# The first x chunk's 1/std on ScalarE and VectorE in place of Pool, with GELU's table loaded behind the last statistics

## The chip, the cores and the metric

The kernel runs on one core of a Trainium2 chip. The metric is the device time of one execution in microseconds (us). Engines are named as in the profile: PE is TensorE (PEld its weight loads), DVE is VectorE, ACT is ScalarE, POOL is GpSimd, SP issues most of the transfers. Times inside an execution count from the start of its span. Runs are called by their labels; "before" and "after" are the two kernels of the change.

The change concerns the first 7 us of 697.

## The reference, cut to what matters

`x` has 2048 tokens of 1024 elements, in 16 chunks of 128 tokens (one token to a partition). It is normalised twice; the doubly normalised `h` feeds a token-mixing MLP, the singly normalised one an attention block.

```python
def _layernorm(x, axis=-1, eps=1e-05):
    m = jnp.mean(x, axis=axis, keepdims=True)
    v = jnp.var(x, axis=axis, keepdims=True)
    return (x - m) / jnp.sqrt(v + eps)
# in _B_ref: h = _layernorm(xn); u = gelu(einsum('bsd,sf->bdf', h, w1) + b1); y = einsum('bdf,fs->bds', u, w2) + b2
# xn = _layernorm(x); return x + _A_ref(xn, ...) + _B_ref(xn, ...)      (A attention, B MLP)
```

The MLP contracts over tokens, so its first matmuls can start as soon as chunk 0 of `h` and the first rows of `w1` are there. They then need one more chunk of `h` every 8 matmuls.

## The kernel before: the parts that matter

`h` of chunk c is `(x - mean) * rs`, with `rs` the power -0.5 of the variance plus a constant `E_H`. Even chunks have their statistics from VectorE (`bn_stats`, two halves, then `bn_aggr`), odd ones from two passes of ScalarE. A string gives the order in which work is put on the engines: D and d are VectorE statistics (D all of a chunk, d its first half, d' the second half and `bn_aggr`), A and A' ScalarE's two passes, S is `rs`, h is the scaling, C the bias columns. Each engine gets its own list from this string; in the traces VectorE and ScalarE take theirs in that order.

```python
    NORM_ORDER = (["D0 A1 S0 d2 h0 A1' A3 S1 d2' h1"] +
                  [f"S{c} d{c + 2} h{c} A{c + 1}' A{c + 3} S{c + 1} d{c + 2}' h{c + 1}" for c in range(2, 14, 2)] +
                  ["S14 h14 A15' S15 C h15"])

    def rstd(self, c):                       # "S"
        ...
        fw.op("dve", ... tensor_scalar(var, ..., E_H, op0=ALU.mult, op1=ALU.add) ...)
        fw.op("pool", ... tensor_tensor(rs, var, self.expo[:, 0:1], op=ALU.pow) ...)

    def early_hidden(self, c0, c1, bank_groups):       # 8 matmuls for each chunk, 4 for each half of h
        ...
            reads = self.R_w1e[c0:c1] + self.R_w1s[0:2] + self.R_hh[banks[0] % 2][c0:c1]
```

## Time and profile before

The three runs took 697.14, 697.40 and 697.45 us.

| what | value | view |
|---|---|---|
| span of the profiled execution | 695.2 us | page |
| TensorE busy | 685.3 us | page, part 1 |
| matmul's share of the chain that ended last | 98% | page, part 4 |
| first real matmul | 6.83 us | timeline |

The page of before, part 1 (busy us, share of the span, number of instructions) and part 4 (the chain of waits that ended last, by engine and by line):

```profile
PE 685.3 (99%) x4746; PEld 326.5 (47%) x4830; DVE 257.2 (37%) x581; ACT 280.2 (40%) x333; POOL 100.1 (14%) x156
...
PE 98%; issue 1%; DMA 1%; DVE 0%; SPq 0%
PE ps_all L194 98%; DMA xin<-in_A_x_dram 1%; SPq L216 0%; DVE ln_st L617 0%; DVE h L656 0%; DVE fin L1050 0%; PE ps_all L200 0%
```

Once the matmuls have begun they bound everything; a change to the normalisation pays only if they begin earlier and are then fed in time. The timeline of before around their beginning (start us, length us, engine, line, operation, output and inputs, count; in brackets the idle time before and what ended it):

```profile
5.05 0.21 DVE L620 BATCH_NORM_AGGREGATE ln_mv<-ln_st 128x2 f32<-128x12 f32 x1
5.29 0.15 DVE L639 TENSOR_SCALAR ln_mv<-ln_mv 128x1 f32<-128x1 f32 x1
5.53 0.55 POOL L641 TENSOR_TENSOR ln_rs<-ln_mv,expo 128x1 f32<-128x1 f32 x1 [3.96 <-DVE ln_mv L639]
5.67 0.69 DVE L617 BATCH_NORM_STATS2 ln_st<-xin 128x6 f32<-128x512 bf16 x1 [0.23 <-DMA xin<-in_A_x_dram]
6.29 0.72 DVE L656 TENSOR_SCALAR h<-xin,ln_mv,ln_rs 128x512 bf16<-128x512 bf16 x2
6.80 3.15 PEld L194 LDWEIGHTS ps_all<-h,w1early 128*128 128x128 bf16 x16 [2.00 <-DMA w1early<-in_B_w_dram]
6.83 17.43 PE L194 MATMUL ps_all<-h,w1early 128*128 128x512 bf16 x79 [1.51 <-DVE h L656]
6.92 0.14 DVE L639 TENSOR_SCALAR ln_mv<-ln_sm 128x1 f32<-128x1 f32 x1
7.14 0.55 POOL L641 TENSOR_TENSOR ln_rs<-ln_mv,expo 128x1 f32<-128x1 f32 x1 [1.07 <-DVE ln_mv L639]
7.83 0.68 DVE L656 TENSOR_SCALAR h<-xin,ln_mv,ln_rs 128x512 bf16<-128x512 bf16 x2
```

The first five lines are chunk 0: statistics, the added constant, Pool's power, then `h`, with a `bn_stats` of chunk 2 squeezed in front of `h`. The last three are the add, power and `h` of chunk 1. Its first half ends at 8.19, and the matmuls of chunk 1 begin at 8.55, without a gap behind the eight of chunk 0: `h` is ready about 0.2 us before it has to be, as a matmul starts some 0.15 us after the end of its `h` (the first ones here: 6.69 to 6.83).

### The profile page before, as it was taken

The page shows a single profiled execution, that of the slowest core. Times are in us where ns is not written, and L with a number is a line of the kernel's source. Part 1 is how long each engine was busy: PE and PEld are TensorE (multiplying, and loading weights), DVE is VectorE, ACT ScalarE, POOL GpSimd, SP SyncE. Part 2 cuts the span into 40 slices and gives each one's busy share as a digit, 9 for nine tenths or more (in the row PEclk, how much of TensorE's full clock was granted, in tenths as well). Part 3 has the DMA queues.
Part 4 walks back from the last instruction along what each step waited for, and adds up shares of the span by engine and source line. Part 5 has one row for each costly group of instructions (what it writes and reads, how often), then busy time and mean ns, then how long its engine had stood idle before and what let it go on. Part 6 is the DMA issues. An engine that isn't in the chain of part 4 may idle for free.

```text
span 695.2 us, 11228 instructions
## 1 busy us (share of the span) xinstructions
PE 685.3 (99%) x4746; PEld 326.5 (47%) x4830; DVE 257.2 (37%) x581; ACT 280.2 (40%) x333; POOL 100.1 (14%) x156
## 2 busy tenths in 40 slices
PE   8999999999999999999999999999999999999998
PEld 3444444444444444444444454444444444445454
DVE  6740000000011334334436455536445553434445
ACT  7622222111134444444545444454544444534440
POOL 2600000000001111211121211112121111121130
DMA  9497685226045536645263544626273544436014
GB/s 315 110 221 175 149 227 124 74 60 140 1 138 116 111 65 133 117 107 124 49 126 97 118 95 88 129 47 137 66 148 80 97 95 73 98 63 151 9 31 137
DMA packets 210537, 77.17 MB, mean 111 GB/s; under 512 B 173112, under 2 KB 202808, under 8 KB 210488
## 3 DMA queue, kind: packets, MB, share of 16 engines
q1 hardware_dynamic: 210344, 76.42, 47.9%
q8 instruction: 38, 0.62, 0.4%
q14 instruction: 11, 0.09, 0.0%
q10 hardware_dynamic: 144, 0.03, 0.0%
HBM read 59.79 MB, written 5.24 MB: 94 GB/s over the span
## 4 chain that ended last, share of the span: by engine, by line
PE 98%; issue 1%; DMA 1%; DVE 0%; SPq 0%
PE ps_all L194 98%; DMA xin<-in_A_x_dram 1%; SPq L216 0%; DVE ln_st L617 0%; DVE h L656 0%; DVE fin L1050 0%; PE ps_all L200 0%
## 5 line engine op out<-in xcount | busy, mean ns | idle before, releaser
L194 PE MATMUL ps_all<-gT,w2h 128*128 128x512 bf16 x868 | 207.8, 380 | 1.6 <-issue 0.2
L810 ACT ACTIVATE pT<-ps_all 128x512 bf16<-128x512 f32 (+1 forms) x128 | 151.4, 1235 | 76.7 <-PE ps_all L194 76.7
L194 PE MATMUL ps_all<-h,w1s 128*128 128x512 bf16 x752 | 165.1, 379 | 0.8
L805 POOL TENSOR_SCALAR_AFFINE_SELECT pT<-pT 128x512 bf16<-128x512 bf16 x128 | 83.6, 677 | 557.3 <-ACT pT L810 557.3
L194 PEld LDWEIGHTS ps_all<-gT,w2h 128*128 128x128 bf16 x896 | 83.2, 98 | 105.6 <-issue 13.8
L194 PEld LDWEIGHTS ps_all<-h,w1s 128*128 128x128 bf16 x768 | 75.1, 98 | 90.6
L844 DVE CAST ost<-ps_all 128x264 bf16<-128x264 f32 (+1 forms) x128 | 49.2, 398 | 169.4 <-PE ps_all L194 169.4
L712 ACT ACTIVATE gT<-ps_all,b1c 128x512 bf16<-128x512 f32 x56 | 37.7, 689 | 138.4 <-PE ps_all L194 132.8
L754 DVE CAST kT<-ps_all 128x512 bf16<-128x512 f32 x32 | 22.0, 687 | 176.5 <-PE ps_all L194 176.5
L194 PE MATMUL ps_all<-xnT,wk 128*128 128x512 bf16 x256 | 60.5, 379 | 0.0
L194 PE MATMUL ps_all<-xnT,wq 128*128 128x512 bf16 x256 | 60.4, 378 | 0.0
L194 PEld LDWEIGHTS ps_all<-vA,pT 128*128 128x128 bf16 x1280 | 47.7, 96 | 22.7
L194 PE MATMUL ps_all<-wv_sb,xnT 128*128 128x512 bf16 x227 | 54.0, 379 | 1.6
L738 ACT ACTIVATE qT<-ps_all 128x512 bf16<-128x512 f32 x32 | 19.1, 597 | 78.4 <-PE ps_all L194 78.4
L194 PE MATMUL ps_all<-vA,pT 128*128 128x33 bf16 x1280 | 48.6, 177 | 0.0
L950 DVE SCALAR_TENSOR_TENSOR stg<-ps_all,b2c,stg 128x512 bf16<-128x512 f32 x32 | 24.0, 750 | 61.7 <-PE ps_all L194 61.6
L757 ACT ACTIVATE etmp<-kT 128x512 bf16<-128x512 bf16 x24 | 15.1, 629 | 59.0 <-DVE kT L754 59.0
L194 PEld LDWEIGHTS ps_all<-xnT,wk 128*128 128x128 bf16 x256 | 23.8, 98 | 23.1
L194 PEld LDWEIGHTS ps_all<-wv_sb,xnT 128*128 128x128 bf16 x256 | 23.5, 97 | 23.7
L194 PEld LDWEIGHTS ps_all<-xnT,wq 128*128 128x128 bf16 x256 | 23.4, 97 | 23.2
L772 ACT ACTIVATE vA<-ps_all 128x512 bf16<-128x512 f32 x32 | 19.2, 599 | 37.2 <-PE ps_all L194 37.2
L194 PE MATMUL ps_all<-qT,kT 32*128 32x384 bf16 (+3 forms) x512 | 31.9, 299 | 0.0
(70 smaller groups left out, 419.2 us busy)
## 6 DMA issues: line engine op xcount, KB each, us to landing
w2h<-in_B_w_dram SPq DMA_DIRECT2D x32, 448.0 KB, 4.8
w1s<-in_B_w_dram SPq DMA_DIRECT2D x12, 1024.0 KB, 5.7
wq<-in_A_wq_dram SPq DMA_DIRECT2D x32, 256.0 KB, 4.2
wk<-in_A_wk_dram SPq DMA_DIRECT2D x32, 256.0 KB, 5.0
stg<-in_A_x_dram SPq DMA_DIRECT2D x16, 256.0 KB, 2.9
out_dram<-stg SPq DMA_DIRECT2D x16, 256.0 KB, 2.0
xin<-in_A_x_dram SPq DMA_DIRECT2D x2, 1024.0 KB, 10.5
wv_sb<-in_A_wv_dram SPq DMA_DIRECT2D x2, 1024.0 KB, 8.7
```

The source lines that it names most:

```text
L194: ins = self.nc.tensor.matmul(*args, **kwargs)
L712: fw.op("act", lambda e: e.activation(self.gT[:, fc, half * 512:(half + 1) * 512], self.bank(b), ACT.Gelu_apprx_tanh, bias=self.b1c[:, fc: ...
L738: fw.op("act", lambda e: e.activation(self.qT[k][:], self.bank(b), ACT.Copy), reads=[self.R_bank[b]], writes=[self.R_qT[k]])
L754: fw.op("dve", lambda e: e.tensor_copy(self.kT[k][:], self.bank(b)), reads=[self.R_bank[b]], writes=[self.R_kT[k]])
L757: fw.op("act", lambda e: e.activation(self.etmp[1][:], self.kT[k][:], ACT.Exp), reads=[self.R_kT[k]], writes=[self.R_etmp[1]])
L772: fw.op("act", lambda e: e.activation(self.vA[i][:, c, :, 0:D_HEAD], self.bank(b).rearrange("p (h d) -> p h d", d=D_HEAD), ACT.Copy), read ...
L805: fw.op("pool", lambda e: e.affine_select(d, d, pattern=[[0, 4], [1, P]], compare_op=ALU.is_ge, fill=0.0, base=0, channel_multiplier=-1), ...
L810: self.fw.op("act", lambda e: e.activation(dst, src, ACT.Exp, scale=SCALE), reads=R_src, writes=R_dst)
L844: fw.op("dve", lambda e: e.tensor_copy(dst, self.ps[:, b, 0:n * VW]), reads=[self.R_bank[b]], writes=[self.R_ost[o][qb]])
L950: fw.op("dve", lambda e: e.scalar_tensor_tensor(dst, self.bank(b), self.b2c[:, c:c + 1], dst, op0=ALU.add, op1=ALU.add), reads=[self.R_ban ...
```

## The change

For chunk 0, Pool's power and the VectorE add in front of it go. ScalarE takes the square root of variance plus constant in one instruction, VectorE the reciprocal. The table loaded at the start (1.28 us from 0.80) is now Sqrt's, and GELU's is loaded behind the last statistics pass. The order moves too: chunk 2's first `bn_stats` now comes behind `h` of chunk 0, and chunk 0's add, which a later step still needs, comes last.

```diff
-        fw.op("act", lambda e: e.activation(self.junk[:, 0:1], self.warm[:, 0:1], ACT.Gelu_apprx_tanh),
-              reads=[self.R_warm], writes=[self.R_junk])
+        self.load_table(ACT.Sqrt)
 ...
+        fw.op("pool", lambda e: e.memset(self.e_h[:], E_H), reads=[self.R_expo], writes=[self.R_expo])
 ...
-    NORM_ORDER = (["D0 A1 S0 d2 h0 A1' A3 S1 d2' h1"] +
+    NORM_ORDER = (["D0 A1 Q0 h0 A1' A3 d2 S1 d2' h1 V0"] +
 ...
-                  ["S14 h14 A15' S15 C h15"])
+                  ["S14 h14 A15' G S15 C h15"])
 ...
+    def rstd_sqrt(self, c):                                       # "Q"
+        fw = self.fw
+        rs = self.ln_rs[:, c, 1:2]
+        fw.op("act", lambda e: e.activation(rs, self.ln_mv[:, c, 1:2], ACT.Sqrt, bias=self.e_h[:]),
+              reads=[self.R_st[c], self.R_expo], writes=[self.R_rs[c]])
+        fw.op("dve", lambda e: e.reciprocal(rs, rs), reads=[self.R_rs[c]], writes=[self.R_rs[c]])
```

(The add is now a function of its own, "V", which "S" calls too; "G" loads GELU's table by a one-element activation.)

More of the change, by code (lines that the diff above doesn't have):

```diff
@@ L395, in alloc @@
         self.expo = a.take("expo", [P, N_TCH], F32)
+        self.e_h = a.take("e_h", [P, 1], F32)
         self.ln_sm = a.take("ln_sm", [P, N_TCH, 1], F32)
@@ L521, in consts @@
         self.R_w1e = [Res(f"w1e{c}") for c in range(N_TCH)]
-        fw.op("act", lambda e: e.activation(self.junk[:, 0:1], self.warm[:, 0:1], ACT.Gelu_apprx_tanh),
-              reads=[self.R_warm], writes=[self.R_junk])
-        for kind, c0, n in (("x", 0, 1), ("x", 1, 1), ("x", 2, 1), ("w", 0, 2), ("x", 3, 1), ("x", 4, 2), ("w", 2, 2), ("x", 6, 2),
-                            ("w", 4, 4), ("x", 8, 4), ("w", 8, 4), ("x", 12, 4), ("w", 12, 4)):
+        self.load_table(ACT.Sqrt)
+        for kind, c0, n in (("x", 0, 1), ("x", 1, 1), ("x", 2, 1), ("w", 0, 2), ("x", 3, 1), ("x", 4, 2), ("w", 2, 2),
+                            ("x", 6, 2), ("w", 4, 4), ("x", 8, 4), ("w", 8, 4), ("x", 12, 4), ("w", 12, 4)):
             if kind == "x":
@@ L547, in consts, with load_table @@
                 fw.mm(self.bank(0), self.warm[:, 0:P], self.warm[:], start=True, stop=True)
+    def load_table(self, func):
+        self.fw.op("act", lambda e: e.activation(self.junk[:, 0:1], self.warm[:, 0:1], func), reads=[self.R_warm],
+                   writes=[self.R_junk])
     def bias_columns(self):
@@ L604, in norm_and_first_hidden @@
                 self.rstd(c)
+            elif kind == "Q":
+                self.rstd_sqrt(c)
+            elif kind == "V":
+                self.add_e_h(c)
+            elif kind == "G":
+                self.load_table(ACT.Gelu_apprx_tanh)
             else:
@@ L637, in rstd, with add_e_h @@
         fw = self.fw
-        R, var, rs = self.R_st[c], self.ln_mv[:, c, 1:2], self.ln_rs[:, c, 1:2]
-        fw.op("dve", lambda e: e.tensor_scalar(var, self.ln_sm[:, c, :] if c % 2 else var, 1.0 / D_MODEL if c % 2 else 1.0,
-                                               E_H, op0=ALU.mult, op1=ALU.add), reads=[R], writes=[R])
-        fw.op("pool", lambda e: e.tensor_tensor(rs, var, self.expo[:, 0:1], op=ALU.pow), reads=[R, self.R_expo],
-              writes=[self.R_rs[c]])
+        self.add_e_h(c)
+        fw.op("pool", lambda e: e.tensor_tensor(self.ln_rs[:, c, 1:2], self.ln_mv[:, c, 1:2], self.expo[:, 0:1],
+                                                op=ALU.pow), reads=[self.R_st[c], self.R_expo], writes=[self.R_rs[c]])
+    def add_e_h(self, c):
+        var = self.ln_mv[:, c, 1:2]
+        self.fw.op("dve", lambda e: e.tensor_scalar(var, self.ln_sm[:, c, :] if c % 2 else var,
+                                                    1.0 / D_MODEL if c % 2 else 1.0, E_H, op0=ALU.mult, op1=ALU.add),
+                   reads=[self.R_st[c]], writes=[self.R_st[c]])
+    def rstd_sqrt(self, c):
[4 more added lines that the diff above has]
+        fw.op("dve", lambda e: e.reciprocal(rs, rs), reads=[self.R_rs[c]], writes=[self.R_rs[c]])
     def rstd_first(self):
```

## The prediction

> **What bounds the kernel now.** TensorE: 685.3 of 695.2 us busy (page, part 1), and the chain of waits is matmul for 98%. Only the head before the first real matmul, at 6.83 us, and the last output lie outside. So the change pays only by starting matmuls earlier, fed without a new gap.
>
> **The head of the chain, from the timeline.** bn_aggr of chunk 0 ends at 5.26; the VectorE add runs 5.29-5.45; Pool's pow 5.53-6.08 (0.55); meanwhile VectorE has started chunk 2's first bn_stats (5.68-6.37), released by its DMA, so h of chunk 0 starts at 6.29, not at about 6.18; its first half ends at 6.68; first matmul 6.83.
>
> **The change, costed.**
> - Removed for chunk 0: the add (0.15) from the chain, Pool's pow (0.55), and the bn_stats in front of h (0.11 of delay).
> - Added: a one-column Sqrt. The one-column warm-up ACTIVATE took 0.21; a pointer bias costs 0.09 (1.15 against 1.06 for the two statistics passes); estimate 0.30, 5.31 (behind chunk 1's first pass) to 5.61. A one-column reciprocal: 16 and 32 columns took 0.25 and 0.35; estimate 0.15, ending near 5.82.
> - h of chunk 0 then starts near 5.85, its first half ends near 6.25: 0.43 earlier.
> - Table load: the trace shows 1.28 us at the start and again at 203 us[...]. The first load only changes its set; the new GELU load falls near 25 us, and ScalarE is idle there until 31.63. Cost nothing. [...]
>
> **How much reaches the end.** Two things eat the 0.43:
> 1. The first matmul also waits for w1 chunks 0-1. Their DMA landed at about 6.55 (the landing records), so the matmul starts near 6.61: gain 0.22.
> 2. Chunk 1. Before, its matmuls began at 8.55 without a gap; h was 0.22 ahead of need (8.19). Now chunk 2's bn_stats stands between h0 and chunk 1's add, and ScalarE's second pass of chunk 1 comes about 0.08 later. Estimate: add 7.10 (was 6.92), pow 7.32-7.88, h1 from 8.00, first half done 8.37, matmul possible at 8.51, wanted at 8.33. A new gap near 0.18, and chunk 1 starts only 0.04 earlier than before.
> From chunk 2 on VectorE waits for chunk 4's DMA (8.85), as before, and nothing later changes.
>
> Net: 0.04 us gained, perhaps 0 to 0.2, inside the spread of the three runs (0.31).
>
> **Prediction: 697.3 us, 8 in 10 between 696.7 and 697.9.** Faster by over 2%: 0.003; within 2%: 0.992; slower: 0.005.
>
> **What would show each step.** Sqrt near 5.3, 0.3 long; reciprocal 0.15; h0 from 5.85; the first weight load released by w1's DMA, not by h, and the first matmul at 6.6; a matmul gap of about 0.2 before chunk 1, released by VectorE's h; chunk 2's first matmul within 0.1 of before (10.27); two table loads before 30 us; the first GELU still waiting for TensorE.
>
> **What would make it wrong.** A smaller gap at chunk 1 leaves up to 0.2 us of gain; Sqrt queueing behind the accumulator read, or a slow one-column reciprocal, makes the gap bigger and the change slower by 0.1 to 0.2; [...]a different DMA order shifts w1's landing. None is near 2%.

(The forecast came to 0.04 us gained, 0.22 at the first matmul less the new gap of 0.18 at chunk 1.)

## More of the kernel before

At the start come ten matmuls on zeros, the warm-up (`N_WARM = 10`; most of them start 0.427 us apart in before, the real ones behind them 0.216), and the transfers are issued in this order (kind, first chunk, number of chunks):

```python
        for kind, c0, n in (("x", 0, 1), ("x", 1, 1), ("x", 2, 1), ("w", 0, 2), ("x", 3, 1), ("x", 4, 2), ("w", 2, 2), ...
```

## The result, and the profile after

| | runs | median us | lowest to highest |
|---|---|---|---|
| before | 6 | 697.27 | 696.95 to 698.75 |
| after | 6 | 698.18 | 696.92 to 699.24 |

The ratio of after to before is 1.0009, with a 95% interval of 0.9995 to 1.0024: the same. A ratio here is the mean time of one kernel's runs over that of the other's of the same rounds, so it is not quite the ratio of the medians.

The medians differ by 0.9 us all the same, and after's lies outside the range that was predicted. The profiled execution of after was one of 699.24 us, 2.3 us over the profiled one of before. Its timeline, the lines that answer to those of before:

```profile
5.33 0.29 ACT L662 ACTIVATE ln_rs<-ln_mv,e_h 128x1 f32<-128x1 f32 x1
5.66 0.16 DVE L664 RECIPROCAL ln_rs<-ln_rs 128x1 f32<-128x1 f32 x1 [0.36 <-ACT ln_rs L662]
5.86 0.73 DVE L678 TENSOR_SCALAR h<-xin,ln_mv,ln_rs 128x512 bf16<-128x512 bf16 x2
6.51 0.69 DVE L628 BATCH_NORM_STATS2 ln_st<-xin 128x6 f32<-128x512 bf16 x1
7.11 0.14 DVE L655 TENSOR_SCALAR ln_mv<-ln_sm 128x1 f32<-128x1 f32 x1
7.33 0.55 POOL L650 TENSOR_TENSOR ln_rs<-ln_mv,expo 128x1 f32<-128x1 f32 x1 [5.60 <-DVE ln_mv L655]
7.42 0.55 PEld L194 LDWEIGHTS ps_all<-h,w1early 128*128 128x128 bf16 x4 [2.73 <-DMA w1early<-in_B_w_dram]
8.08 0.68 DVE L678 TENSOR_SCALAR h<-xin,ln_mv,ln_rs 128x512 bf16<-128x512 bf16 x2
```

VectorE and ScalarE do what was intended: `h` of chunk 0 starts at 5.86, not at 6.29. But TensorE waits until 7.42 for the first rows of `w1`. By the landing records, their transfer was complete at 7.38, against 6.55 in before, although it was issued at the same time (2.2 us) in both. Fifteen of its sixteen parts had landed by 6.56; one came 0.8 us later.

That explains 0.6 us of the 2.3. The rest is in the clock. The view by stretches, before (for each stretch: us, then busy us and instruction count of each engine, then the granted clock of TensorE, the transfer share and GB/s):

```profile
8.00:11.40 3.40, 3.40 (x18) 1.51 (x17) 3.09 (x11) 3.25 (x7) 1.10 (x2) 1.00 1.07 382
```

and after:

```profile
8.00:11.40 3.40, 3.40 (x10) 1.22 (x8) 2.85 (x10) 3.21 (x5) 1.10 (x2) 0.51 1.07 381
11.40:14.80 3.40, 3.40 (x18) 1.53 (x16) 3.08 (x10) 3.24 (x7) 1.17 (x3) 1.00 1.06 378
```

PE is "fully busy" in both, but it gets through 18 matmuls in before and 10 in after, at a granted clock of 0.51. (The trace of before has no clock records, and then the view's column shows 1.00 whatever the clock was, as over the 11 matmuls of before_warm4 below; for before the 18 matmuls, 0.216 us from start to start, are the evidence of full speed.) Eight matmuls of 0.216 us each (the first eight of before take from 6.83 to 8.55) are 1.7 us. Together: 0.6 + 1.7 = 2.3 us, the whole difference of the two spans (697.5 and 695.2). After's clock records give full clock from 4.53 and half clock from 7.94 to 11.36 us, each 3.413 us long.

In before TensorE idled 1.51 us between the warm-up and its first real matmul, in after 2.24, mostly because `w1` was late, and all of it inside the stretch of full clock that ended at 7.94. That the idle time brought the clock down, one pair of traces does not show.

So the profiled pair doesn't measure the change: it compares an undisturbed head with a disturbed one. The question for the experiments was whether the change makes the disturbance, and what it is worth without it.

### The profile page after: what moved, and what is told of

Same layout as the page of the kernel before. It is cut to its first block, busy times and chain, and to the rows that moved or that the text cites. A ratio compares the mean times of both kernels' runs of the same rounds, so it can differ in the third digit from the quotient of the medians.

```text
span 697.5 us, 11232 instructions
## 1 busy us (share of the span) xinstructions
PE 686.9 (98%) x4746; PEld 326.8 (47%) x4830; DVE 257.4 (37%) x582; ACT 281.8 (40%) x336; POOL 99.6 (14%) x156
## 4 chain that ended last, share of the span: by engine, by line
PE 98%; DMA 1%; issue 1%; SPq 0%; DVE 0%
PE ps_all L194 98%; DMA w1early<-in_B_w_dram 1%; SPq L216 0%; DVE fin L1072 0%; PE ps_all L200 0%
```

## The experiments

The two theories. A: the 0.9 us is chance, from the landing of `w1` and from whether the clock is at half in the head; the change itself is worth about nothing, because what it gains at the first matmul it gives back at chunk 1. B: the change itself makes the head slower or the half clock more frequent.

The tally of slow heads counts runs over 698 us. That limit was set after the first runs were seen: most lie below 697.9 and another group between 698.3 and 699.4.

### The changed kernel once more

The edit is none.

> The changed kernel once more, unaltered. Theory A (chance): the 0.9 us between the medians came from two things that differ from one execution to the next and that the change does not touch: when the last of the 16 parts of w1's first transfer lands (6.55 us in the trace of before, 7.38 in that of after) and whether TensorE's clock falls to half in the head (in the trace of after it was 0.5 from 8.13 to 11.55 us). Then before shows slow runs too, the ratio's interval covers 1, and both kernels have runs near 697 and runs of 698.5 to 699.3. Theory B (the change does it): after stays 0.5 to 1 us above before, whose runs stay at 697.0 to 697.5.

(The times 8.13 to 11.55 in that text were taken against the wrong zero; they are 7.94 to 11.36, as above.)

Measured: after 697.02 us median of 5 (696.84 to 698.84), before 697.34 of 9 (696.93 to 699.16), ratio 0.9998 (0.9984 to 1.0011). This time before has two runs over 698 and after one. Theory B's expectation failed. And the profiled execution, of 697.02 us, had a head at full clock, so it is the one to set beside before. Its timeline:

```profile
5.38 0.29 ACT L662 ACTIVATE ln_rs<-ln_mv,e_h 128x1 f32<-128x1 f32 x1
5.71 0.16 DVE L664 RECIPROCAL ln_rs<-ln_rs 128x1 f32<-128x1 f32 x1 [0.36 <-ACT ln_rs L662]
5.91 0.74 DVE L678 TENSOR_SCALAR h<-xin,ln_mv,ln_rs 128x512 bf16<-128x512 bf16 x2
6.56 0.69 DVE L628 BATCH_NORM_STATS2 ln_st<-xin 128x6 f32<-128x512 bf16 x1
6.60 1.41 PEld L194 LDWEIGHTS ps_all<-h,w1early 128*128 128x128 bf16 x8 [1.81 <-DMA w1early<-in_B_w_dram]
7.17 0.14 DVE L655 TENSOR_SCALAR ln_mv<-ln_sm 128x1 f32<-128x1 f32 x1
8.14 0.68 DVE L678 TENSOR_SCALAR h<-xin,ln_mv,ln_rs 128x512 bf16<-128x512 bf16 x2
8.55 1.41 PEld L194 LDWEIGHTS ps_all<-h,w1early 128*128 128x128 bf16 x8 [0.54 <-DVE h L678]
```

The whole argument of the prediction is in these lines. The first weight load is at 6.60, released by the transfer of `w1` (landed 6.56) and no longer by `h`. Then chunk 1's add waits behind chunk 2's `bn_stats` until 7.17 (6.92 in before), its `h` starts at 8.14 (7.83), and TensorE stands still until 8.55, released by that `h`. Chunk 1's matmuls begin at 8.55 in before as well. The 0.22 us gained at the first matmul is gone 2 us later. At chunk 2 the first matmul comes at 10.38, 0.10 later than in before (10.28), and the span is longer by the same 0.1 (695.3 against 695.2). But x chunk 0 had landed 0.09 us later in this execution (3.66 against 3.57), and VectorE's whole list with it. So the balance of the change itself is zero to within 0.1 us, and its sign cannot be had from one execution of each. Nor from the runs under 698 us: after's median of these was 0.4 us above before's in the first rounds (697.51 and 697.14) and 0.3 below in these (697.02 and 697.32).

### A longer warm-up, in both kernels

```diff
-    N_WARM = 10
+    N_WARM = 14
```

> Before with 14 warm-up matmuls in place of 10. The warm-up then ends near 6.1 us instead of 5.3, and TensorE idles at most 1.4 us before its first real matmul even if w1 lands as late as 7.4. Theory A: the clock never falls in the head, no run above 698, median 696.9 to 697.5, unchanged from before in its fast runs. If the clock has nothing to do with the spread, slow runs of 698.5 and over are as frequent as before.

> After with 14 warm-up matmuls. Theory A: the clock never falls in the head; median within 0.3 us of before_warm14, about 697.0 to 697.4, since what the change gains at the first matmul is given back at chunk 1. In the profile the gap before chunk 1 is about 0.2 us if w1 landed near 6.55, none if it landed after about 6.8. Theory B: still 0.5 to 1 us above before_warm14.

Measured on the same chip: before_warm14 697.50 (697.08 to 697.69, 5 runs), after_warm14 697.41 (697.05 to 697.63, 5 runs). No run of the ten is over 698; of before's nine in the same rounds two are. The two kernels differ by 0.09 us in their medians, well inside their spread. Theory A's numbers hold, at the upper edge of its ranges; theory B's 0.5 to 1 us is not there. The traces also show the price: in the profiled after_warm14 the clock rose late, at 6.82, so 14 matmuls at half speed kept TensorE until 7.02, past the landing of `w1` (6.57). In before_warm14's a transfer was late (x chunk 2 at 6.37), so `h` of chunk 0, behind that chunk's `bn_stats`, started only at 7.00: the order of before does have that weakness. It also separates the two causes of lateness: its first matmul came at 7.54, 0.7 us later than in before, but at full clock, and that run took 697.62 us. In this execution, late transfers alone did not make a run of over 698.

### A shorter warm-up, to call the half clock up

```diff
-    N_WARM = 10
+    N_WARM = 4
```

> Before with 4 warm-up matmuls in place of 10, to call the half clock up on purpose. The warm-up ends near 3.0 us and TensorE idles some 3.8 us before its first real matmul. Theory A: the clock is at half for the first matmuls, for something between one and two of the 3.41 us steps seen in the trace of after, and every us at half costs half a us: 1.7 to 3.4 us slower than the runs at full clock, all runs 698.8 to 700.8, with almost no spread between fast and slow runs. If the clock isn't the cause of the slow runs: median near 697.3.

Measured: 699.51 us (698.93 to 699.76, 4 runs), before 697.42 in the same rounds; ratio 1.0024 (1.0007 to 1.0040). All four runs are slow, 2.1 us by the medians, as expected. The view by stretches of before_warm4:

```profile
8.00:11.40 3.40, 3.40 (x11) 1.30 (x10) 3.23 (x10) 3.24 (x7) 1.12 (x3) 1.00 1.05 373
```

Eleven matmuls where before has 18: half speed for most of the stretch. The column of the granted clock says 1.00 here, though, as this trace, too, has no clock records. The matmul count is the reading to trust. It also shows another way to a slow head than that of after: the matmuls stand some 0.427 us apart from the first of the warm-up until 10.5, so no matmul before that shows a clock that had risen and could fall.

### The two halves of the change, one at a time

The new order alone, Pool's power kept:

```diff
-    NORM_ORDER = (["D0 A1 S0 d2 h0 A1' A3 S1 d2' h1"] +
+    NORM_ORDER = (["D0 A1 S0 h0 A1' A3 d2 S1 d2' h1"] +
```

> Before with the new order alone: chunk 2's first bn_stats behind h of chunk 0, Pool's pow kept. My theory: h of chunk 0 starts near 6.18 (before 6.29), first matmul near 6.73 (before 6.83), but the add of chunk 1 goes behind bn_stats, its pow to about 7.65-8.2, its h first half is ready near 8.67 and chunk 1 starts near 8.80 after a gap of 0.35: 0.25 us later than before. Times 697.2 to 697.8 in runs at full clock. Rival (order is what gains): first matmul as early and no gap.

Measured: 697.33 us (697.16 to 698.61, 4 runs; one over 698). The timeline of the profiled execution, which was at full clock:

```profile
6.11 0.73 DVE L656 TENSOR_SCALAR h<-xin,ln_mv,ln_rs 128x512 bf16<-128x512 bf16 x2 [0.75 <-POOL ln_rs L641]
6.70 1.90 PE L194 MATMUL ps_all<-h,w1early 128*128 128x512 bf16 x8 [1.40 <-DMA w1early<-in_B_w_dram]
7.37 0.14 DVE L639 TENSOR_SCALAR ln_mv<-ln_sm 128x1 f32<-128x1 f32 x1
8.34 0.68 DVE L656 TENSOR_SCALAR h<-xin,ln_mv,ln_rs 128x512 bf16<-128x512 bf16 x2
8.76 5.59 PE L194 MATMUL ps_all<-h,w1early 128*128 128x512 bf16 x25 [0.16 <-DVE h L656]
```

First matmul 6.70 (expected 6.73), chunk 1 from 8.76 (expected 8.80) after a gap of 0.32 (expected 0.35), 0.21 later than in before. (A gap is counted here and below from start to start, less the 0.216 us of one matmul.) The span, 695.4, is longer by 0.2. And x chunk 0 had landed 0.08 us earlier here than in before (3.49), so the order alone costs some 0.2 to 0.3 us: chunk 1's add waits behind `bn_stats` while nothing has been gained yet by a faster 1/std.

The square root alone, in the old order:

```diff
-    NORM_ORDER = (["D0 A1 Q0 h0 A1' A3 d2 S1 d2' h1 V0"] +
+    NORM_ORDER = (["D0 A1 Q0 d2 h0 A1' A3 S1 d2' h1 V0"] +
```

> After with the old place of chunk 2's first bn_stats (between the reciprocal and h of chunk 0). My theory: h of chunk 0 waits for bn_stats as in before and starts near 6.43, first matmul near 6.95, so Sqrt alone gains nothing at the head; chunk 1's h comes in time (about 8.4 for a need at 8.67) and there is no gap before chunk 1. Chunk 1 starts 0.1 us later than before, times 697.0 to 697.6 in runs at full clock.

Measured: 697.40 us (697.07 to 698.68, 4 runs; one over 698). In its trace `h` of chunk 0 starts at 6.41, the first weight load is at 6.92, and the first half of chunk 1's `h` ends at 8.32, all close to what was expected: in the old order Sqrt alone puts the first matmul 0.1 us later than before (x chunk 0's landing at 3.66 is 0.09 of that), so it gains nothing at the head. The profiled execution was the one of 698.68 us, whose matmuls ran at half speed from the first one on:

```profile
8.00:11.40 3.40, 3.40 (x11) 1.24 (x10) 3.28 (x13) 3.24 (x7) 1.10 (x2) 1.00 1.07 379
```

This trace again has no clock records. By the spacing (0.427 us) all ten warm-up matmuls were at half speed as well, and the clock rose only at about 10.3. TensorE had idled just 1.25 us before its first real matmul, less than in before. So chunk 1's `h` was wanted late, and whether there would be a gap before chunk 1 at full clock this run cannot tell.

### w1's first transfer ahead of x chunk 2

```diff
-        for kind, c0, n in (("x", 0, 1), ("x", 1, 1), ("x", 2, 1), ("w", 0, 2), ("x", 3, 1), ...
+        for kind, c0, n in (("x", 0, 1), ("x", 1, 1), ("w", 0, 2), ("x", 2, 1), ("x", 3, 1), ...
```

> After with w1's first transfer issued ahead of x chunk 2. w1 lands near 5.7 us, so the first matmul is released by h of chunk 0, at about 6.4, 0.43 us before that of before. My theory of chunk 1: its h is ready no earlier than with the change alone, first matmul of chunk 1 near 8.55 after a gap of about 0.45 us, so the 0.4 us are given back in full: median 696.9 to 697.4. The rival, that VectorE makes chunk 1's h in time: gap under 0.1, chunk 1 starts near 8.15, 0.4 us gained to the end. A late part of w1's transfer no longer matters, so few runs over 698.

Measured: 697.23 us (697.13 to 697.54, 5 runs, none over 698). From its timeline:

```profile
6.33 7.85 PE L194 MATMUL ps_all<-h,w1early 128*128 128x512 bf16 x32 [0.64 <-DVE h L678]
6.74 0.69 DVE L628 BATCH_NORM_STATS2 ln_st<-xin 128x6 f32<-128x512 bf16 x1 [0.23 <-DMA xin<-in_A_x_dram]
7.35 0.14 DVE L655 TENSOR_SCALAR ln_mv<-ln_sm 128x1 f32<-128x1 f32 x1
8.32 0.68 DVE L678 TENSOR_SCALAR h<-xin,ln_mv,ln_rs 128x512 bf16<-128x512 bf16 x2
```

The first matmul comes at 6.33, half a us before that of before, released by `h` now. And all of it is given back: chunk 1's `h` starts at 8.32 and its first matmul at 8.74, 0.2 us later than in before. x chunk 2 has become the late transfer (6.72), its `bn_stats` holds VectorE's list, and chunk 1's add stands behind it. The rival, that VectorE would be in time, fell. The gap before chunk 1 is 0.28, not the expected 0.45, because the first three matmuls still ran at half speed: in this execution the clock rose only at 7.18.

The same transfer order without Sqrt (the new order of work, Pool's power kept):

> Before with the new order and with w1's first transfer ahead of x chunk 2, and Pool's pow kept: what the transfer order gives without Sqrt. First matmul near 6.7, released by h (w1 has landed), a gap of 0.3 to 0.4 us before chunk 1, which starts near 8.8. If the order of the transfers is what takes the slow runs away, no run over 698 and median 697.1 to 697.6; if Sqrt is needed for that (TensorE idles 0.35 us longer than with it), slow runs remain, about one in three.

Measured: 697.93 us (697.24 to 698.81, 6 runs), three over 698; before in the same rounds five of eleven. The transfer order alone doesn't take the slow runs away. The first weight load at 6.73 and that of chunk 1 at 8.85, behind a gap of 0.37, are as expected.

### Feeding chunks 1 and 2 in time

To see whether the late `h` is what gives the gain back, Sqrt and reciprocal were used for chunks 1 and 2 as well, on top of the transfer order:

```diff
-    NORM_ORDER = (["D0 A1 Q0 h0 A1' A3 d2 S1 d2' h1 V0"] +
-                  [f"S{c} d{c + 2} ..." for c in range(2, 14, 2)] +
+    NORM_ORDER = (["D0 A1 Q0 h0 A1' d2 Q1 A3 i1 d2' j1 Q2 h2 V0 V1 V2 A3' A5 d4 S3 d4' h3"] +
+                  [f"S{c} d{c + 2} ..." for c in range(4, 14, 2)] +
```

(i and j are the first and the second half of h. Cut: the functions for these, and the transfer order.)

> After with w1's first transfer ahead of x chunk 2, and with 1/std of chunks 1 and 2 by Sqrt and reciprocal too, the two halves of chunk 1's h on either side of a bn_stats. If the late h of chunks 1 and 2 is what gives the gain back: first matmul near 6.35, no gap over 0.15 us before chunk 1, 2 or 3, so the matmuls are 0.3 to 0.5 us ahead of before at chunk 4 (less what a half clock in the first matmuls costs): 696.7 to 697.0 in runs at full clock. If something else gives it back, the matmuls of chunk 4 start within 0.1 us of before.

Measured: 697.11 us (696.99 to 697.76, 6 runs, none over 698), before 697.42 in the same rounds with five of eleven over 698; ratio 0.9993 (0.9979 to 1.0007). From its timeline:

```profile
6.29 7.91 PE L194 MATMUL ps_all<-h,w1early 128*128 128x512 bf16 x33 [0.59 <-DVE h L681]
7.50 0.41 DVE L681 TENSOR_SCALAR h<-xin,ln_mv,ln_rs 128x512 bf16<-128x512 bf16 x1
9.31 0.55 DVE L681 TENSOR_SCALAR h<-xin,ln_mv,ln_rs 128x1024 bf16<-128x1024 bf16 x1
10.56 0.14 DVE L657 TENSOR_SCALAR ln_mv<-ln_sm 128x1 f32<-128x1 f32 x1
11.54 0.49 DVE L681 TENSOR_SCALAR h<-xin,ln_mv,ln_rs 128x1024 bf16<-128x1024 bf16 x1
```

Chunk 1 now has its `h` from 7.50 (8.14 in after_again) and no gap; chunk 2's gap is under 0.1 us. But chunk 3's add comes only at 10.56 (9.90 in before), behind what was put in front of it, its `h` starts at 11.54, and TensorE waits there by 0.2 us (11.65 to 12.09, start to start). The first three matmuls here, too, ran at half speed, until 7.11. From chunk 4 on the matmuls run 0.1 us later than in before. My expectation (0.3 to 0.5 us ahead) missed; by the numbers it is the other outcome. The cause of the gap at chunk 1 is shown, since making that `h` earlier removed it, but the loss then moved on to chunk 3. And among the runs under 698 us fed's median (697.11) is not below that of before in the same rounds (696.96).

A second try put chunk 3 on Sqrt too, moved the additions to the end and used 12 warm-up matmuls:

> The second try at feeding the early chunks: as the run fed, with chunk 3's 1/std by Sqrt and reciprocal too, placed ahead of the next chunk's statistics, the four additions moved to the end, and 12 warm-up matmuls, which close the idle time before the first real matmul to about 1 us. If h of the next chunk is what gave the gain back each time: no gap before chunks 1, 2 and 3, perhaps 0.2 to 0.3 us before chunk 4, and chunk 5 starts 0.1 to 0.4 us earlier than in before (15.24): 696.7 to 697.1, and no run over 698. If the loss only moves on to a later chunk once more, chunk 5 starts within 0.1 us of before or later.

Measured: 697.65 us (697.02 to 698.56, 6 runs, one over 698), before 697.98 of 11 in the same rounds; ratio 0.9993 (0.9977 to 1.0008). In the profiled execution x chunk 3 landed at 8.49 (7.34 in before), ScalarE's pass over it started late, and everything behind it in ScalarE's list, chunk 2's square root included, with it: a gap of 1.0 us before chunk 2 (matmuls from 10.77), and chunk 5 began at 16.28, 0.8 us later than in before (15.46; the 15.24 in the text above is the last matmul of chunk 4, whose record is missing). The expectation missed, and one run was slow where none was expected. The gain that I wanted to show is still not shown. What this run shows is that more square roots in ScalarE's list tie more chunks to one late transfer.

### GELU's table without the explicit load

```diff
-                  ["S14 h14 A15' G S15 C h15"])
+                  ["S14 h14 A15' S15 C h15"])
```

> After without the explicit load of GELU's table, so that the load comes where the first GELU needs it. My theory that the early load buys nothing in time: the load stands at about 31.5 us, 1.28 us long, the first GELU ends 1.3 us later than in after, and TensorE shows no gap near 34 us, because its first reuse of a bank comes over 1 us after that; the time is that of after at the same clock. Rival (it hides a wait): a gap in the matmuls of up to 1 us near 34 us.

Measured (one look): 697.12 us, correct. The timeline of after_again at that place:

```profile
24.89 1.28 ACT L551 ACT_TABLE_LOAD   x1
26.18 0.20 ACT L551 ACTIVATE junk<-warm 128x1 bf16<-128x1 bf16 x1
31.73 4.73 ACT L734 ACTIVATE gT<-ps_all,b1c 128x512 bf16<-128x512 f32 x8 [5.34 <-PE ps_all L194]
```

and of gelu_late:

```profile
25.21 1.28 ACT L734 ACT_TABLE_LOAD   x1
31.82 4.73 ACT L734 ACTIVATE gT<-ps_all,b1c 128x512 bf16<-128x512 f32 x8 [5.32 <-PE ps_all L194]
```

The expectation missed, in a useful way. The load that the compiler placed for the first GELU here didn't wait for what GELU waited for. It ran as soon as ScalarE had finished its statistics, at 25.2 us, 6.6 us before the GELU. Both theories had assumed otherwise; the explicit load buys nothing, not even an earlier table.

### The version meant to beat both

After with `w1` first and `N_WARM = 12`:

> The version meant to beat both: the change, w1's first transfer ahead of x chunk 2, and 12 warm-up matmuls, so that TensorE idles under 1.2 us before its first real matmul. If the slow runs come from idle time before the first real matmul: no run over 698, all within 0.7 us, median 696.9 to 697.4, and the ratio to before at or just below 1, since about one run in three of before is slow. If they come from elsewhere: one or two runs of six over 698.

Measured: 697.65 us (697.18 to 697.86, 5 runs, none over 698), before on that chip 698.80 (697.27 to 699.41, 9 runs, seven over 698); ratio 0.9984, interval 0.9971 to 0.9998. It is the only run whose interval leaves 1 out on the fast side, by 0.16%, far under the 2% that would count as faster. The gain comes from having no slow heads: its median is no better than the two runs of before under 698 (697.27 and 697.42). Its profiled execution shows why not more was to be had. x chunk 2 landed at 7.15, and chunk 1's matmuls began at 9.17 after a gap of 0.9 us, released by `h`. Which part the change, the transfer order and the two warm-up matmuls have in this was not separated.

The tally of runs over 698 us, over all rounds (without before_warm4, slow by design in 4 of 4, and gelu_late, one run):

| kernels | runs over 698 |
|---|---|
| before | 20 of 46 |
| after (both times) | 4 of 11 |
| reorder_only, sqrt_only, reorder_w1first | 5 of 14 |
| before_warm14, after_warm14 | 0 of 10 |
| after_w1first, fed, fed2_warm12, after_w1first_warm12 | 1 of 22 |

The rate differs by chip (two of before's nine runs on one, seven of nine on another), and kernels were compared within the same rounds. In those rounds the last two groups had 1 of 32, and before 19 of 40. Both groups shorten the time that TensorE idles between warm-up and work, by different means: more warm-up, or an earlier first matmul. The kernels that do neither, or only a little of it, have slow runs at a rate like that of before. That fits theory A. Not every slow run has a trace. That each of them had a half clock is argued from the three that have one (after, sqrt_only, before_warm4) and from the mean clock of 0.997 or 0.998 that some others list; it is not shown. Why the chips differ stays open.

The idle time is not the whole of it, though. In after the clock had risen (4.53) and fell again (7.94); in sqrt_only and before_warm4, as far as the matmuls show, it had not risen by the first real matmul, and in sqrt_only that cost the head with only 1.25 us of idle time. In reorder_w1first 1.71 us idle (5.05 to 6.76), behind a rise at 4.25, cost nothing. So when the clock rises seems to count as well, and over the nine traces that record it this moment lies anywhere between 4.25 (reorder_w1first) and 7.18 us (after_w1first). More warm-up, or earlier matmuls, also put more matmuls into the first 7 us; the runs don't separate that from the shorter idle time. What makes the clock rise or fall is not shown, and no limit of idle time was measured.

## Why the prediction was right or wrong

1. **The bound.** Right: TensorE's chain decides, and of the head, as long as the clock is full, only the start of the matmuls and the gaps in them count. The spans of after_again and reorder_only differ from that of before by just the amount (0.1 and 0.2 us) by which their early matmuls are late.
2. **Costs of the pieces.** Right. Sqrt estimated at 0.30 from 5.31: measured 0.29 from 5.33. Reciprocal estimated at 0.15: 0.16. `h` of chunk 0 predicted at 5.85: 5.86.
3. **The first matmul held by w1.** Right: predicted 6.61, measured 6.60 in after_again, released by the transfer. That it agrees to 0.01 is luck: the transfer landed at 6.56 in this execution, as in before, but between 6.55 and 7.38 over the nine traces with its old place in the order.
4. **The gain given back at chunk 1.** Right. Predicted: a new gap of 0.18 and chunk 1 at 8.51, 0.04 before that of before. Measured in after_again: a gap of 0.21 and 8.55, level with before, in an execution whose x chunk 0 was 0.09 late.
5. **"nothing later changes".** Half right. The prediction had VectorE wait for a transfer at chunk 2 as before; in after_again it didn't, it was still behind from chunk 1, and chunk 2's `h` began at 9.69 (9.46 in before). The matmuls of chunk 2 started 0.10 later than in before: at the edge of the 0.1 that was allowed, and no more than the late landing. The predicted sum, 0.04 us gained, is below what these runs can tell from zero.
6. **The table loads.** The cost of nothing was right. After has two loads before 30 us (1.28 us each, from 0.80 and from 25.60) and none between, so the table loaded for Sqrt served the Identity and Square of the statistics passes as well. The activation behind each of the two starts 0.01 us after the load's end (2.085 to 2.096, 26.885 to 26.896). That the explicit load was needed was taken for granted; gelu_late shows that it isn't.
7. **The spread.** This is the step that failed, a size and not the mechanism of the change. The prediction called the gain small against "the spread of the three runs (0.31)". All three were of the fast group. Over 46 runs before spreads from 696.87 to 699.41 us, and 20 are over 698. So the range of 696.7 to 697.9 did not hold after's median of 698.18. Over all 11 runs after's median is 697.51, inside it. The prediction named a shifted landing of `w1` among what could go wrong; it did not think of the clock, which in the profiled execution of after, with that transfer 0.8 us and the first matmul 0.6 us late, added 1.7 us to the 0.6 by its stretch at half speed.

So: "same" and the mechanism stand, point by point; the time missed its range on the first six runs because of run-to-run slow heads that the change, as far as these runs show, does not cause.

## What to carry to other kernels

A gain at the head of a chain is worth only what the next consumer can use: before shortening the first link, look up how far ahead of need the second and third are (here 0.2 us), because an engine that works through one list in order pays for what was moved behind (here chunk 1's add on VectorE, at 7.17 in after_again and at 6.92 in before). When two medians differ by less than the spread, look first at whether the two profiled executions were in the same condition, by the transfers' landings and by the number of matmuls in a fixed stretch (a clock column of 1.00 can mean that nothing was recorded, as with the 11 matmuls of before_warm4); 1.7 of the 2.3 us here were a clock at half speed for 3.4 us. And time more than three runs before calling their spread the spread.
